# Chunked attention, a two-dimensional DFT and an MLP on one core: the PSUM banks divided among the three, and attention regrouped

## The chip, the cores and the metric

The kernel runs on one core of a Trainium2 chip. The metric is the device time of one execution in microseconds, as the median of several. Times before: 495.82, 498.5 and 500.54 us, median 498.5.

## What is computed

The reference first does attention in chunks of 32 positions, each with 16 positions to its left, 8 to its right and 8 memory positions, over 4 batches, 8 heads, 768 positions and a head size of 64. The heads side by side are x (4 x 768 x 512), and then:

```python
X = np.fft.fft(x, axis=1)
X = np.fft.fft(X, axis=2)
u = x + np.real(X).astype(np.float32)
mu = np.mean(u, axis=-1, keepdims=True)
var = np.mean((u - mu) ** 2, axis=-1, keepdims=True)
un = (u - mu) / np.sqrt(var + 1e-06)
ch = np.maximum(un @ w_ch1, 0.0) @ w_ch2        # 512 -> 2048 -> 512
return (u + ch).astype(np.float32)
```

## The kernel before

**Attention** (emit_pair, line 222) works on a pair of heads, 4 pairs a batch, 16 in all. The loads of q, k and v go through SP's queue (emit_loads, lines 105 to 120) into buffers that alternate: two for q and k, four for v (two pairs). POOL casts q and k to bf16 (lines 231, 233) and copies the overlap of v (line 237). PE transposes q and k (lines 242, 247) into one PSUM tile trp, ACT copies them out as qT and kT (lines 244, 252). PE then makes the scores of both heads in 24 matmuls (line 259) into two tiles sc0 and sc1 of two banks each; for each head ACT takes the exponential in two instructions (line 266), PE multiplies with v, in 12 products over tile xa (line 271; a product in fp32 shows as two matmul records), and DVE divides by the sum of weights (lines 274, 276) into xsb, which holds x of the batch. There are two xsb buffers: attention of batch b+2 writes into the one that the MLP of batch b reads last (line 379).

**The Fourier stage** (emit_fx, line 281), called so below, folds x by its symmetries on DVE (lines 290 to 299: zy, pq, ff), splits it into two fp16 parts hi (ACT, line 303) and lo (DVE, line 304), and does the DFT over positions as 60 matmuls of 193 columns into ps (lines 312, 319), which ACT and DVE take out as up and dn (lines 326 to 329). Then comes a loop kt over 6 blocks of 128 positions (line 333): 8 matmuls of the DFT over channels into pm (line 341), DVE adds x (xsb, line 345), does the statistics (lines 347, 348) and subtracts the mean (un, line 350), PE transposes un into tp (line 353), DVE copies it to unT (line 354). pm of kt 0 to 2 reads up, that of kt 3 to 5 reads dn. POOL makes rstd from the variances at the end (lines 356, 357).

**The MLP** (emit_mlp, line 360) runs over two halves of 384 positions. For each half there are 16 groups ht of 4 matmuls into ph (line 368), each followed by relu on ACT into hT (line 371), then 3 blocks of 16 matmuls into pc (line 376), each followed by osb on DVE (line 379) and an output DMA on SP's queue (line 381). The first half of positions needs unT of kt 0 to 2 alone.

**Order and buffers.** The order in which instructions stand on each engine is made by a scheduler that goes by a model of times and, among what could run, by the order of the text: attention 0, Fourier 0, attention 1, Fourier 1, MLP 0, attention 2, Fourier 2, MLP 1 and so on. On the chip every engine and every queue then keeps that order. A tile takes its buffer in the order of the text as well. The 8 banks of PSUM are divided so: trp, sc0 and sc1 share two buffers of two banks under the tag "sc" (4 banks), xa has one bank, and the tag "acc" of the pool fps has three, which the tiles mps, ps, pm, tp, ph and pc share. The weights of the MLP are loaded by eight DMAs on POOL's queue (emit_weights, line 204), in the text behind pair 2.

Of the kernel before, what the change touches and what calls it, by code (L numbers as in the profile page):

```python
# [10 lines left out]
FP32 = mybir.dt.float32  # L11
# [24 lines left out]
def kernel(  # L36
# [15 lines left out]
    P = 128  # L52
# [21 lines left out]
    fps = ctx.enter_context(tc.tile_pool(name="fx_ps", bufs=3, space=bass.MemoryType.PSUM))  # L74
# [147 lines left out]
    def emit_pair(n):  # L222
        b, pr = seq[n]
        h = 2 * pr
        if b not in xs:
            xs[b] = apool.tile([P, NST, DM], FP32, tag="xsb", bufs=2, name=f"xsb{b}")
        xb = xs[b]
        emit_loads(n)
        qb = apool.tile([QP, RB, 2, D], BF16, tag="qb", bufs=2)
        kb = apool.tile([KP, RB, 2, D], BF16, tag="kb", bufs=2)  # L230
# [31 lines left out]
        for hh in range(2):
            v1 = va[(2 * n + hh) % NV]
            e1 = apool.tile([P, NT, 64], FP32, tag="e1", bufs=3)
            for c in range(2):
                nc.scalar.activation(e1[:, :, ts(c, 32)], sc[hh][:, :, ts(c, 32)], AFT.Exp,  # L266
                                     bias=mbias[:, c:c + 1], scale=1.0 / math.sqrt(D))
            xa = aps.tile([P, NST, 66], FP32, tag="xa", bufs=1)
# [116 lines left out]
    for i in range(HP):  # L385
        emit_pair(i)
        if i == HP - 2:
            emit_weights()
# [37 lines left out]
```

## Time and profile before

| | us |
|---|---|
| times of three runs | 495.82, 498.5, 500.54 |
| the profiled execution, its own time | 500.56 |
| its span, first to last instruction | 498.6 |
| PE busy in the span | 340.6 (68%) |
| DVE busy | 207.1 (42%) |
| ACT busy | 150.6 (30%) |
| POOL busy | 90.8 (18%) |
| mean granted clock of PE | 0.808 |

PE is the matmul engine, PEld its weight loads, DVE the vector engine, ACT the one for functions, POOL and SP two more that also issue DMAs. "L341" is line 341 of the kernel before; lines move by up to 21 in the kernel after. [...] A busy PE is not a PE at its peak, since matmuls overlap: a matmul's duration is longer than the distance to the next. A matmul record of xa is half a product. All times in the rows are microseconds from the start of the span, unless marked ns.

### The profile page before, as it was taken

Reading aid. Unit: us, or ns where it says so; the run is one execution under the profiler, and the core shown is the slowest. Engines: PE = TensorE matmul, PEld = TensorE weight load, DVE = VectorE, ACT = ScalarE, POOL = GpSimd, SP = SyncE. Lnnn points to the kernel's source line nnn. Section 1 sums busy time; section 2 is a strip of 40 time slices with the busy share of each in tenths; the row PEclk is TensorE's granted clock in tenths of the full one; section 3 lists DMA queues with packets and bytes.
Section 4 is the critical chain, followed back from the end, with each engine's and each line's share of the span. In section 5 each row is a group of like instructions: output and inputs, shape, how many; then the busy total and the mean of one; then the engine's idle time right before and its main releaser. Section 6 shows DMA issues by size and latency. Waiting matters only on the chain.

```text
span 498.6 us, 6910 instructions
## 1 busy us (share of the span) xinstructions
PE 340.6 (68%) x2848; PEld 221.8 (44%) x2848; DVE 207.1 (42%) x365; ACT 150.6 (30%) x258; POOL 90.8 (18%) x99
## 2 busy tenths in 40 slices
PE   1045526766556669996557458997535559999996
PEld 1044415655444445554545235454523335555452
DVE  7911189564595450103186651103495550101101
ACT  2444242213423115233442005160312006244160
POOL 9715157005520013002422001000100010000000
PEclk9999999676556569999756558999757559999999
DMA  9639994332633005104130000102100000101101
GB/s 168 98 91 186 217 185 75 82 77 62 157 77 73 0 1 128 63 21 108 45 79 22 0 0 1 42 22 82 38 0 0 1 0 1 63 21 43 43 21 63
DMA packets 42022, 30.65 MB, mean 61 GB/s; under 512 B 30216, under 2 KB 32264, under 8 KB 41992
## 3 DMA queue, kind: packets, MB, share of 16 engines
q1 hardware_dynamic: 39304, 26.03, 22.7%
q0 software_dynamic: 2688, 4.19, 4.7%
q8 instruction: 22, 0.36, 0.3%
q14 instruction: 8, 0.07, 0.0%
HBM read 28.11 MB, written 6.29 MB: 69 GB/s over the span
## 4 chain that ended last, share of the span: by engine, by line
PE 57%; DVE 22%; DMA 7%; issue 6%; ACT 4%; SPq 2%; POOL 2%; POOLq 0%; ACTq 0%; DVEq 0%
PE ph L368 17%; PE pc L376 17%; PE pm L341 7%; DMA kf<-in_k_dram 6%; PE xa L271 5%; PE ps L312 5%; DVE xsb L345 3%; DVE st L347 3%; PE tp L353 3%; DVE zy L290 2%; DVE lo L304 2%; DVE un L350 2%; DVE xsb L276 1%; PE sc L259 1%; SPq L116 1%
## 5 line engine op out<-in xcount | busy, mean ns | idle before, releaser
L371 ACT ACTIVATE hT<-ph 128x384 f16<-128x384 f32 x128 | 62.9, 491 | 130.8 <-PE ph L368 130.3
L368 PE MATMUL ph<-unT,w_sb 128*128 128x384 f16 x512 | 87.1, 332 | 0.0
L376 PE MATMUL pc<-w_sb,hT 128*128 128x512 f16 x384 | 84.2, 379 | 0.0
L379 DVE SCALAR_TENSOR_TENSOR osb<-pc,rstd,xsb 128x512 f32<-128x512 f32 x24 | 18.0, 751 | 151.6 <-PE pc L376 151.6
L368 PEld LDWEIGHTS <-w_sb 128*128 128x128 f16 x512 | 51.0, 100 | 35.0 <-issue 2.7
L271 PE MATMUL xa<-va,e 128*64 128x65 f32 x768 | 43.9, 285 | 30.4 <-issue 13.2
L376 PEld LDWEIGHTS <-hT 128*128 128x128 f16 x384 | 37.6, 98 | 44.4
L271 PEld LDWEIGHTS xa<-va,e 128*64 128x64 f32 x768 | 38.6, 193 | 36.2 <-issue 22.0
L237 POOL COPY va<-va 32x768 f32<-32x768 f32 x32 | 32.5, 1029 | 100.8 <-DMA va<-in_v_dram 100.1
L266 ACT ACTIVATE e<-sc,mbias 128x384 f32<-128x384 f32 x64 | 32.4, 581 | 48.1 <-PE xa L271 31.1
L353 PE MATMUL tp<-ident_h,un 128*128 128x128 f16 x96 | 13.7, 293 | 39.9 <-DVE un L350 39.8
L312 PE MATMUL ps<-cosS,hi 128*128 128x193 f16 x48 | 15.8, 358 | 25.3 <-ACT hi L303 25.3
L356 POOL TENSOR_SCALAR rstd<-mu_s 128x6 f32<-128x6 f32 x4 | 2.0, 491 | 166.8 <-DVE mu_s L348 166.8
L244 ACT COPY qT<-trp 128x768 bf16<-128x768 bf16 x16 | 12.8, 800 | 62.5 <-PE trp L242 62.5
L259 PE MATMUL sc<-qT,kTb 64*128 64x64 bf16 x384 | 14.1, 224 | 25.0 <-ACT kTb L252 23.8
L353 PEld LDWEIGHTS <-un 128*128 128x128 f16 x96 | 7.8, 125 | 47.4 <-DVE un L350 47.0
L274 DVE RECIPROCAL zs<-xa 128x6 f32<-128x6 f32 x32 | 6.2, 194 | 51.6 <-PE xa L271 51.6
L231 POOL CAST qb<-qf 96x1024 bf16<-96x1024 f32 x16 | 18.7, 1166 | 46.8 <-PE trp L242 41.7
L345 DVE TENSOR_TENSOR xsb<-pm,xsb 128x512 f32<-128x512 f32 x24 | 16.6, 692 | 24.5 <-PE pm L341 24.3
L312 PEld LDWEIGHTS <-hi 128*128 128x128 f16 x96 | 12.7, 139 | 27.7 <-ACT hi L303 26.8
L326 ACT CAST up<-ps 128x386 f16<-128x386 f32 x16 | 9.5, 596 | 49.4 <-PE ps L312 37.8
L259 PEld LDWEIGHTS <-kTb 64*128 64x128 bf16 x384 | 11.0, 116 | 30.1 <-ACT kTb L252 26.6
(92 smaller groups left out, 455.7 us busy)
## 6 DMA issues: line engine op xcount, KB each, us to landing
qf<-in_q_dram SPq DMA_DIRECT2D x16, 384.0 KB
kf<-in_k_dram SPq DMA_DIRECT2D x16, 384.0 KB
out_dram<-osb SPq DMA_DIRECT2D x24, 256.0 KB
va<-in_v_dram SPq DMA_DIRECT2D x32, 144.0 KB
w_sb<-in_moe_w_ch_dram POOLq DMA_DIRECT2D x8, 512.0 KB, 14.0
va<-in_v_dram SPq DMA_DIRECT2D x32, 48.0 KB
va<-in_mem_v_dram SPq DMA_DIRECT2D x32, 24.0 KB
mkf<-in_mem_k_dram SPq DMA_DIRECT2D x1, 64.0 KB
```

What stands on the lines that cost most here:

```text
L231: nc.gpsimd.tensor_copy(qb.rearrange("p j h d -> p h j d"), qf[n % NS].rearrange("p h (j d) -> p h j d", j=RB))
L237: nc.gpsimd.tensor_copy(v1[96:128, 0:NT, 0:D], v1[0:32, 1:NB, 0:D])
L259: nc.tensor.matmul(sc[hh][:, t, :], kT[r0:r0 + 64, t * BS:t * BS + P], qT[r0:r0 + 64, ts(t, 64)], start=True, stop=True, tile_position=(r0 ...
L266: nc.scalar.activation(e1[:, :, ts(c, 32)], sc[hh][:, :, ts(c, 32)], AFT.Exp, bias=mbias[:, c:c + 1], scale=1.0 / math.sqrt(D))
L271: nc.tensor.matmul(xa[rr:rr + 64, t // 2, 0:65], e1[:, t, :], v1[:, t, 0:65], start=True, stop=True)
L312: nc.tensor.matmul(ps[:, sp, :], part[:, ab, sp * 3 + st, :], tab[:, sp, st, :], start=(st == 0 and i == 0), stop=(st == 2 and i == 1))
L341: nc.tensor.matmul(pm[:, par, :], lhs, rhs[:, par, :], start=(im == 0), stop=(im == 3))
L345: nc.vector.tensor_tensor(uv, pm, uv, ALU.add)
L353: nc.tensor.transpose(tp[:, dt, :], un[:, ts(dt, P)], ident_h)
L368: nc.tensor.matmul(ph[:, 0:384], w1_sb[:, dt, ts(ht, P)], unT[:, dt, sh * 384:(sh + 1) * 384], start=(dt == 0), stop=(dt == NDT - 1))
L371: nc.scalar.activation(hT[:, ht, :], ph[:, 0:384], AFT.Relu)
L376: nc.tensor.matmul(pc, hT[:, ht, ts(stl, P)], w2_sb[:, ht, :], start=(ht == 0), stop=(ht == NHT - 1))
```

## The change

Three things. The pool fps has two buffers a tag instead of three, and ph and pc get a tag of their own, "mlp"; so the Fourier stage and the MLP each have two banks. The transposes of q and k move into a function emit_keys, which is called for pair n+1 ahead of emit_pair for pair n; they have a tag "tr" with one bank, which trq and trk use in turn. And a pair is done in two halves g of 6 blocks for both heads at once: one sc tile (tag "sc", one buffer of two banks, a bank a head), two exps, 12 products into one xa tile, one division. The counts of instructions on each engine stay what they were. PSUM is then: tr 1, sc 2, xa 1, acc 2, mlp 2.

```diff
-    fps = ctx.enter_context(tc.tile_pool(name="fx_ps", bufs=3, space=bass.MemoryType.PSUM))
+    fps = ctx.enter_context(tc.tile_pool(name="fx_ps", bufs=2, space=bass.MemoryType.PSUM))
...
-    def emit_pair(n):
+    qT_of, kT_of = {}, {}
+
+    def emit_keys(n):
...
-        trp = aps.tile([P, 2, 1024], BF16, tag="sc", bufs=2)
+        trq = aps.tile([P, S], BF16, tag="tr", bufs=1, name="trq")
...
+        trk = aps.tile([P, RB * KP], BF16, tag="tr", bufs=1, name="trk")
...
+        qT_of[n], kT_of[n] = qT, kT
+
+    def emit_pair(n):
...
-        sc = [aps.tile([P, NT, 64], FP32, tag="sc", bufs=2, name=f"sc{hh}") for hh in range(2)]
-        for t in range(NT):
-            for hh in range(2):
-                r0 = 64 * hh
-                nc.tensor.matmul(sc[hh][:, t, :], kT[r0:r0 + 64, t * BS:t * BS + P],
...
-        for hh in range(2):
-            v1 = va[(2 * n + hh) % NV]
-            e1 = apool.tile([P, NT, 64], FP32, tag="e1", bufs=3)
-            for c in range(2):
-                nc.scalar.activation(e1[:, :, ts(c, 32)], sc[hh][:, :, ts(c, 32)], AFT.Exp,
...
-            xa = aps.tile([P, NST, 66], FP32, tag="xa", bufs=1)
-            for t in range(NT):
-                rr = 64 * (t % 2)
-                nc.tensor.matmul(xa[rr:rr + 64, t // 2, 0:65], e1[:, t, :], v1[:, t, 0:65],
-                                 start=True, stop=True)
...
+        qT, kT = qT_of.pop(n), kT_of.pop(n)
+        for g in range(2):
+            sc = aps.tile([P, 2, 8, 64], FP32, tag="sc", bufs=1, name="sc")
+            for t6 in range(6):
+                t = 6 * g + t6
+                for hh in range(2):
+                    r0 = 64 * hh
+                    nc.tensor.matmul(sc[:, hh, t6, :], kT[r0:r0 + 64, t * BS:t * BS + P],
+                                     qT[r0:r0 + 64, ts(t, 64)], start=True, stop=True,
+                                     tile_position=(r0, 0))
+            e1 = apool.tile([P, 2, 6, 64], FP32, tag="e1", bufs=3, name="e1")
+            for half in range(2):
+                nc.scalar.activation(e1[:, :, :, ts(half, 32)], sc[:, :, 0:6, ts(half, 32)],
+                                     AFT.Exp, bias=mbias[:, half:half + 1],
+                                     scale=1.0 / math.sqrt(D))
+            xa = aps.tile([P, 3, 2, 66], FP32, tag="xa", bufs=1, name="xa")
+            for st in range(3):
+                for hh in range(2):
+                    v1 = va[(2 * n + hh) % NV]
+                    for half in range(2):
+                        t6 = 2 * st + half
+                        nc.tensor.matmul(xa[64 * half:64 * half + 64, st, hh, 0:65],
+                                         e1[:, hh, t6, :], v1[:, 6 * g + t6, 0:65],
+                                         start=True, stop=True)
...
-                ph = fps.tile([P, 512], FP32, tag="acc", name="ph")
+                ph = fps.tile([P, 512], FP32, tag="mlp", name="ph")
...
-                pc = fps.tile([P, DM], FP32, tag="acc", name="pc")
+                pc = fps.tile([P, DM], FP32, tag="mlp", name="pc")
...
+    def emit_attention(b):
+        for i in range(HP):
+            n = b * HP + i
+            if n + 1 < B * HP:
+                emit_keys(n + 1)
+            emit_pair(n)
+            if n == HP - 2:
+                emit_weights()
```

The scheduler makes another order of this. The first place is on PE, in the kt loop of batch 1; tp_1421 and tp_1442 (before) or tp_1423 and tp_1444 (after) are the transposes of two steps that follow each other. Before:

```order
L353 MATMUL tp_1421<-ident_h_125,un_1419 128x128
L341 LDWEIGHTS dn_1279
L341 MATMUL pm_1427<-cosD_148,dn_1279 128x256
...
L341 MATMUL pm_1427<-sinD_150,dn_1358 128x256
L353 LDWEIGHTS un_1440
L353 MATMUL tp_1442<-ident_h_125,un_1440 128x128
```

After, where pc_1811 and pc_1831 are tiles of the MLP of batch 0:

```order
L367 MATMUL tp_1423<-ident_h_125,un_1421 128x128
L355 LDWEIGHTS up_1322
L355 MATMUL pm_1429<-cosD_148,up_1322 128x256
...
L355 MATMUL pm_1429<-nsinD_149,up_1401 128x256
L390 LDWEIGHTS hT_1694
L390 MATMUL pc_1811<-w2_sb_189,hT_1694 128x512
...
L390 MATMUL pc_1831<-w2_sb_189,hT_1694 128x512
L367 LDWEIGHTS un_1442
L367 MATMUL tp_1444<-ident_h_125,un_1442 128x128
```

Between pm of one step and tp of the same block there stood nothing; now there stand 13 matmuls of pc (1 of pc_1811 and 12 of pc_1831).

The second place is on ACT, from the second half of the MLP of batch 0 to the first of batch 1. Before, the relus of a half stand together:

```order
L371 ACTIVATE hT_1650<-ph_1735 128x384
L371 ACTIVATE hT_1650<-ph_1741 128x384
L266 ACTIVATE e1_2067<-sc0_2041,mbias_133 128x12x32 x2
L266 ACTIVATE e1_2086<-sc1_2042,mbias_133 128x12x32 x2
L244 COPY qT_2119<-trp_2120 128x768
```

After, the casts of the Fourier stage (hi, up), the exps (e1) and the copies of attention stand among them:

```order
L385 ACTIVATE hT_1694<-ph_1761 128x384
L317 CAST hi_1305<-ff_1301 128x1536
L385 ACTIVATE hT_1694<-ph_1767 128x384
L385 ACTIVATE hT_1694<-ph_1773 128x384
L275 ACTIVATE e1_1901<-sc_1888,mbias_133 128x12x32 x2
L385 ACTIVATE hT_1694<-ph_1779 128x384
L385 ACTIVATE hT_1694<-ph_1785 128x384
L340 CAST up_1322<-ps_1309 128x2x193
```

What moved are the relus: of the 128 in the kernel, the first 96 (batches 0 to 2) have left their place behind the Fourier stage of the next batch and stand beside it.

The third place is on PE, where the first ps of batch 1 is. Before, xa of the next attention is beside it:

```order
L312 MATMUL ps_1265<-cosS_146,hi_1261 128x193
L312 MATMUL ps_1283<-sinS_147,hi_1261 128x193
L271 MATMUL xa_1872<-va0_80,e1_1869 64x65 x12
L312 LDWEIGHTS lo_1262
L312 MATMUL ps_1265<-cosS_146,lo_1262 128x193
```

After:

```order
L326 MATMUL ps_1309<-cosS_146,hi_1305 128x193
L326 MATMUL ps_1327<-sinS_147,hi_1305 128x193
L382 MATMUL ph_1779<-unT_765,w1_sb_188 128x384
...
L382 MATMUL ph_1785<-unT_765,w1_sb_188 128x384
L284 MATMUL xa_1904<-va0_80,e1_1901 64x65
L326 MATMUL ps_1309<-cosS_146,lo_1306 128x193
```

The wait for lo is filled with two groups of ph of batch 0 and a first product of xa.

## Rows read from the trace of the kernel before

**Rows 1.** The page, busy time of each engine in the span.
```profile
PE 340.6 (68%) x2848; PEld 221.8 (44%) x2848; DVE 207.1 (42%) x365; ACT 150.6 (30%) x258; POOL 90.8 (18%) x99
```

**Rows 2.** Busy time by windows: us, PE, PEld, DVE, ACT, POOL, granted clock, DMA.
```profile
250.00:301.00 51.00, 28.59 (x202) 20.46 (x199) 35.26 (x54) 8.99 (x12) 6.33 (x6) 0.53 0.10 25
301.00:344.00 43.00, 43.00 (x228) 22.50 (x227) 4.18 (x6) 15.72 (x32) 1.35 (x1) 0.97 0.08 31
344.00:361.00 17.00, 9.89 (x209) 8.61 (x208) 6.77 (x17) 5.64 (x10) 2.47 (x3) 0.82 0.23 57
452.00:498.00 46.00, 42.41 (x229) 22.10 (x226) 5.26 (x7) 15.72 (x32) 0.00 (x0) 1.00 0.10 40
```

**Rows 3.** Timeline, kt 2 and 3 of batch 2: start, us, instruction, idle before.
```profile
284.97 0.69 DVE L345 TENSOR_TENSOR xsb<-pm,xsb 128x512 f32<-128x512 f32 x1 [1.28 <-PE pm L341]
...
286.64 0.48 DVE L350 TENSOR_SCALAR un<-xsb,mu_s 128x512 f16<-128x512 f32 x1
...
287.18 0.60 PE L353 MATMUL tp<-ident_h,un 128*128 128x128 f16 x4 [2.25 <-DVE un L350]
...
289.53 0.69 DVE L345 TENSOR_TENSOR xsb<-pm,xsb 128x512 f32<-128x512 f32 x1 [1.28 <-PE pm L341]
```

**Rows 4.** Timelines of DVE and PE, start of the Fourier stage of batch 2.
```profile
251.22 1.76 DVE L290 TENSOR_TENSOR zy<-xsb 128x1536 f32<-128x1536 f32 x1
...
258.96 0.34 PE L312 MATMUL ps<-cosS,hi 128*128 128x193 f16 x1 [1.49 <-ACT hi L303]
...
266.02 0.25 PE L319 MATMUL ps<-cosS,hi 128*1 128x193 f16 x1
266.11 0.24 PE L319 MATMUL ps<-cosS,lo 128*1 128x193 f16 x1
```

**Rows 5.** The chain that ended last: start, us, what.
```profile
101.31 0.89 PE pm L341 x8
...
105.16 1.21 PE pm L341 x8
...
287.79 1.72 PE pm L341 x8
...
323.32 10.40 PE ph L368 x64
333.72 10.36 PE pc L376 x48
...
484.05 10.37 PE pc L376 x48
```

**Rows 6.** Timeline, attention of batch 2 behind the MLP of batch 0.
```profile
229.70 1.05 ACT L266 ACTIVATE e<-sc,mbias 128x384 f32<-128x384 f32 x2 [12.24 <-PE xa L271]
...
230.59 0.92 PE L271 MATMUL xa<-va,e 128*64 128x65 f32 x24 [0.94 <-PE xa L271]
...
231.44 0.51 PE L242 MATMUL trp<-ident_b,qb 96*128 96x96 bf16 x8
...
235.13 0.52 PE L259 MATMUL sc<-qT,kTb 64*128 64x64 bf16 x24
```

**Rows 7.** Timeline of PE, attention of batch 0.
```profile
42.15 0.82 PE L242 MATMUL trp<-ident_b,qb 96*128 96x96 bf16 x8
...
51.98 0.82 PE L242 MATMUL trp<-ident_b,qb 96*128 96x96 bf16 x8
...
60.99 1.57 PE L271 MATMUL xa<-va,e 128*64 128x65 f32 x24 [1.86 <-DMA va<-in_mem_v_dram]
```

**Rows 8.** The page, DMA issues: KB each, median us to landing.
```profile
w_sb<-in_moe_w_ch_dram POOLq DMA_DIRECT2D x8, 512.0 KB, 14.0
```

**Rows 9.** The page, groups of the MLP: busy, mean ns of one, idle before.
```profile
L371 ACT ACTIVATE hT<-ph 128x384 f16<-128x384 f32 x128 | 62.9, 491 | 130.8 <-PE ph L368 130.3
L368 PE MATMUL ph<-unT,w_sb 128*128 128x384 f16 x512 | 87.1, 332 | 0.0
L379 DVE SCALAR_TENSOR_TENSOR osb<-pc,rstd,xsb 128x512 f32<-128x512 f32 x24 | 18.0, 751 | 151.6 <-PE pc L376 151.6
```

More of the change, by code (lines that the diff above doesn't have):

```diff
@@ L220, in emit_mem_keys @@
         nc.vector.tensor_copy(mkT, mps)
-    def emit_pair(n):
+    qT_of, kT_of = {}, {}
+    def emit_keys(n):
         b, pr = seq[n]
[L224 to L227, printed above, removed]
         emit_loads(n)
-        qb = apool.tile([QP, RB, 2, D], BF16, tag="qb", bufs=2)
-        kb = apool.tile([KP, RB, 2, D], BF16, tag="kb", bufs=2)
+        qb = apool.tile([QP, RB, 2, D], BF16, tag="qb", bufs=2, name="qb")
+        kb = apool.tile([KP, RB, 2, D], BF16, tag="kb", bufs=2, name="kb")
         nc.gpsimd.tensor_copy(qb.rearrange("p j h d -> p h j d"),
@@ L238, in emit_pair @@
         kT = kTb[n % NKT]
-        qT = apool.tile([P, S], BF16, tag="qT", bufs=2)
-        trp = aps.tile([P, 2, 1024], BF16, tag="sc", bufs=2)
+        qT = apool.tile([P, S], BF16, tag="qT", bufs=2, name="qT")
+        trq = aps.tile([P, S], BF16, tag="tr", bufs=1, name="trq")
         for j in range(RB):
-            nc.tensor.transpose(trp[:, 0, j * QP:(j + 1) * QP],
+            nc.tensor.transpose(trq[:, j * QP:(j + 1) * QP],
                                 qb[:, j].rearrange("p h d -> p (h d)"), ident_b[0:QP, 0:QP])
         nc.scalar.copy(qT.rearrange("p (a j) -> p a j", j=RB),
-                       trp[:, 0, 0:S].rearrange("p (j a) -> p a j", j=RB))
+                       trq.rearrange("p (j a) -> p a j", j=RB))
+        trk = aps.tile([P, RB * KP], BF16, tag="tr", bufs=1, name="trk")
         for j in range(RB):
-            nc.tensor.transpose(trp[:, 1, j * KP:(j + 1) * KP],
+            nc.tensor.transpose(trk[:, j * KP:(j + 1) * KP],
                                 kb[:, j].rearrange("p h d -> p (h d)"), ident_b[0:KP, 0:KP])
@@ L262, in emit_pair @@
[L262 to L277 removed]
+            strided(trk, 0, [[8, NB], [1, 8], [KP, RB]]))
@@ new lines, in emit_keys @@
+        qT_of[n], kT_of[n] = qT, kT
+    def emit_pair(n):
+        b, pr = seq[n]
+        h = 2 * pr
+        if b not in xs:
+            xs[b] = apool.tile([P, NST, DM], FP32, tag="xsb", bufs=2, name=f"xsb{b}")
+        xb = xs[b]
+        qT, kT = qT_of.pop(n), kT_of.pop(n)
[22 more added lines that the diff above has]
+                                         start=True, stop=True)
+            zs = apool.tile([P, 3, 2], FP32, tag="zs", bufs=3, name="zs")
+            nc.vector.reciprocal(zs, xa[:, :, :, 64])
+            nc.vector.tensor_tensor(
+                xb[:, 3 * g:3 * g + 3, h * D:(h + 2) * D].rearrange("p s (h d) -> p s h d", h=2),
+                xa[:, :, :, 0:D], zs.unsqueeze(3).to_broadcast([P, 3, 2, D]), ALU.mult)
@@ L383 @@
     HP = H // 2
+    def emit_attention(b):
[6 more added lines that the diff above has]
+                emit_weights()
     emit_mem_keys()
[L385 to L388, printed above, removed]
+    emit_keys(0)
+    emit_attention(0)
     emit_fx(0)
@@ L391 @@
         if b + 1 < B:
-            for i in range(HP):
-                emit_pair((b + 1) * HP + i)
+            emit_attention(b + 1)
             emit_fx(b + 1)
```

8 lines of the change are left out of this document (removed).

## The prediction

> **What bounds the kernel now.** I read the page's busy shares first: PE is busy for 340.6 us of the span, 68%, the other engines less [rows 1], so no engine fills the span and the stages have to be looked at one by one. The table of windows does that for one batch [rows 2]. In the Fourier stage of batch 2 (250 to 301 us) PE is busy 28.6 of 51 us at a granted clock of 0.53, and DVE 35.3. In the MLP of batch 1 (301 to 344) PE is full, at 0.97, and DVE does 4.2 us. In the attention of batch 3 (344 to 361) PE has 9.9 of 17 us. So the stages have opposite limits and stand one behind the other: the Fourier stage is a chain PE to DVE to PE, the MLP is PE alone, and the last 46 us are again MLP alone.
>
> The timeline shows the chain. One step of the kt loop (line 333) goes from the start of xsb at 284.97 to the next at 289.53, 4.56 us; PE starts tp at 287.18, after 2.25 us of idling for un, which DVE ended at 287.12 (286.64 + 0.48) [rows 3]. Ahead of the loop stand 7.7 us of DVE and ACT, zy at 251.22 to the first ps at 258.96 [rows 4]. From that ps to the end of the pm of kt 3 (just ahead of the xsb at 289.53, which reads it: its pm is the first that reads dn) it takes 30.6 us [rows 3, 4]. The MLP of a batch needs unT of kt 0 to 2 alone to begin, but its PSUM tiles come from the same three "acc" banks as the Fourier tiles of the next batch, in the order of the text; so it stands behind that whole stage.
>
> **Prices on PE.** [...] At the fast level: 64 ph matmuls 10.40 us, 0.1625 each; 48 pc 10.36, 0.216 each [rows 5]; 12 products of xa 0.92, 8 transposes 0.51, 24 sc 0.52 [rows 6]; ps 0.09 each (266.02 to 266.11) [rows 4].
>
> **What the change does, part by part.**
>
> *Attention alone (batch 0).* No instruction is added: 24 sc, 24 xa products, 4 exps, 16 transposes a pair as before. What changes is the order: two halves with one sc tile, so the second sc half waits for the exps of the first. Before, a pair takes 9.83 us (trp at 42.15 and at 51.98), and the last xa ends at 62.6 [rows 7]. In the new order the key transposes of pair n+1 still stand right ahead of its sc, since trk has to wait for the copy of trq out of the one "tr" bank; only the query half has moved under xa. Of the steps between, what goes is one exp wait and the qT wait, what comes is the wait of the second sc half: I count 8.9 us a pair, so 3 us less over the first four pairs, attention 0 ends near 60. The bounds are no gain (62.6) and 2 us a pair (54).
>
> *Queues.* On POOL the eight weight loads now stand behind the casts and va copies of pair 3, some 10 us later; a load lands in 14.0 us [rows 8], and the first MLP comes at 100, so this costs nothing unless the loads take over 40 us. On SP the outputs of the MLP now stand between the loads of q and k of the next pairs. These loads are issued one pair, thus 10 us of PE work or more, ahead of their use; the xa at 60.99 had waited 1.86 us for one [rows 7]. I take nothing here and keep 2 us a batch for the range.
>
> *From the end of attention 0 to the first MLP.* In the new order ph of batch 0 stands behind the pm of kt 3. Before, that pm ends at 106.4 (105.16 + 1.21) [rows 5], 43.8 us after attention. The same way in batch 2, without attention between, takes 7.7 + 30.6 = 38.3 [rows 3, 4]. I take 41, and the first ph at 101.
>
> *The cycle.* From here on the MLP of batch b fills PE under the attention and the Fourier stage of batch b+1. I cut the new PE order into three stretches a cycle, from the first ph of one batch to that of the next. *A*: kt 3 to 5 of the Fourier stage, three steps. At the fast level a step is shorter by 0.83 of pm and some 0.1 of tp, 3.6; so 10.8 to 13.7, I take 12. PE has 9.2 to 9.9 us of work there, which fits under it. *B*: the main part of the MLP with attention between. By counts from the order and the prices above: cycle 0 has 94 ph, 48 pc, 46 xa, 36 sc and 32 transposes, 32.0 us; cycle 1 has 110, 57, 55, 58 and 32, 37.7; cycle 2 has 102, 65, 48, 48 and 16, 36.4. *C*: the first ps to the pm of kt 3 of the next batch, 30.6 before; at the fast level three pm groups are shorter by 0.9 each with tp, the second 22 ps by 0.07 each, 4.4 together, and three osb of 0.75 [rows 9] come to DVE inside the chain, 2.2: 28.4. PE has 16 to 24 us of work there, and nothing ready for the rest.
>
> *What the split costs.* ph now has two banks where it had three. A bank is held from the first of 4 matmuls to the end of relu: 3 x 0.1625 + 0.33 (mean of an ph matmul) + 0.49 relu [rows 9], with handovers of 0.06 as from un to tp (287.12 to 287.18) [rows 3] on both sides 1.43 us, where two groups of PE work are 1.30. So 0.06 us a group, 1.4 to 1.7 us in each B. ACT also does two exps of 1.05 together [rows 6] and the qT and kT copies between the relus. Each of these can hold ph back by its length less the PE work beside it: between 0 and 8 us in a B (about eight such pieces), I take 3, since sc and xa of the same pair stand beside most of them.
>
> [...]
>
> *The end.* The last MLP has 39 ph under kt 3 to 5 (12 us), then 89 ph and 96 pc, 35.2 with 1.3 for the banks, 36.5. Behind the last pc the span had 4.2 us left (498.6 less 484.05 + 10.37) [rows 5], and keeps them.
>
> **The sum**, against the profiled execution (500.56 us, span 498.6, so 2.0 outside): first ph 101.3; cycle 0 12 + 32.0 + 4.4 + 28.4 = 76.8; cycle 1 12 + 37.7 + 4.7 + 28.4 = 82.8; cycle 2 12 + 36.4 + 4.5 + 28.4 = 81.3; end 12 + 36.5 + 4.2 = 52.7. Together 394.9, with what lies outside 396.9. The profiled execution stood 2.1 above the median of 498.5, so 395 for the median. Before, the way from the pm of kt 3 of batch 0 to the end took 392 us; now it takes 294. The 98 us are not removed work: they are three MLPs of 41.5 us, of which some 25 to 30 each now lie under the chains of the next batch, and PE matmuls that run at the fast level because PE idles less.
>
> **The rivals.** *R1, the cover is better*: fast steps in A (10.8), no ACT stalls in B, the osb in DVE's gaps in C (26), first stretch 38.3. That is 1.2 x 4 + 3 x 3 + 2.4 x 3 + 2.7 less, 24 us: 371. For it: DVE idles 1.28 a step for pm [rows 3]. Against it: ACT and DVE work in order, and each has more kinds of work in a row than before.
>
> *R2, PE's queue gives the chains' waits to the MLP*: the order is fixed, so an sc, xa or tp that comes later than it was placed for stops the ph behind it. Then A keeps 13.7, C 33 (30.6 and the osb), B has 8 of ACT stalls, and 2 more for late loads: 13.3 a cycle and 4 more at the start and the end, some 44: 439. For it: the 2.25 us a step that tp waits for un even now [rows 3]; against it, each such wait has PE work placed ahead of it in the new order.
>
> *R3, slower*: the MLP loses the fast level. It has it before because nothing interrupts it: 0.97 to 1.00 granted, where the Fourier stage with its idle steps has 0.53 [rows 2]. Interleaved, the MLP has the steps' idling in its middle. [...] Against it: the attention of batch 3 with 7 of 17 us idle still has 0.82 [rows 2], and B has next to no idling. [...]
>
> *R4, no change*: the order overlaps on paper, but loads or ACT hold every cycle to its old length of some 111 us (51 + 43 + 17) [rows 2]; about 490.
>
> **How the numbers follow.** My forecast, 380 to 412 by the stalls in B and the steps: 0.55. R1 0.2, R2 0.2, R3 0.02, R4 0.03. The range leaves out half of R1 below and about a third of R2 with R3 and R4 above: 372 to 434. Within 1% is about what a measurement of this kernel can tell from no change: faster 0.96, same 0.02, slower 0.02.
>
> **What would show it right or wrong.** Windows of the changed kernel: no stretch of 40 us with PE full and DVE nearly idle but the last; first ph near 101 us, then cycles of 77 to 83; granted clock over 0.9 in B; ph groups 0.65 to 0.71 apart where nothing stands between; kt steps of 3.6 to 4.6 us. Cycles of 90 or more with PE waiting on ACT's relu or exps say R2; ph matmuls 0.32 us apart with a low clock say R3; a first ph at 106 or later says that the loads or the pair order were wrong.

## The result, and the profile after

The kernel after takes 374.92 us (median of 4 runs, 373.94 to 378.14); the kernel before, run beside it, 497.16 (494.35 to 500.54). The ratio is 0.755, 95% interval 0.748 to 0.762: faster by about 122 us. The prediction had said 395, in a range of 372 to 434. The profiled execution of the kernel after takes 373.94 us, with a span of 372.2.

The page of the kernel after, busy times and three groups of the MLP, to set beside [rows 1, 9]:

```profile
PE 301.9 (81%) x2848; PEld 187.8 (50%) x2848; DVE 196.2 (53%) x365; ACT 148.6 (40%) x258; POOL 84.3 (23%) x99
...
L382 PE MATMUL ph<-unT,w_sb 128*128 128x384 f16 x512 | 96.0, 330 | 1.3 <-DVE osb L393 0.8
L385 ACT ACTIVATE hT<-ph 128x384 f16<-128x384 f32 x128 | 61.9, 494 | 76.8 <-PE ph L382 76.8
...
L393 DVE SCALAR_TENSOR_TENSOR osb<-pc,rstd,xsb 128x512 f32<-128x512 f32 x24 | 17.9, 748 | 51.5 <-PE pc L390 51.5
```

The work on PE hasn't become less (the same 2848 matmuls), yet PE is busy for 302 us where it was 341: the same matmuls run at the higher clock level more of the time (the mean granted clock, a share of PE's full clock in the trace, is 0.980, where it was 0.808). The relus, which waited 130.3 us for ph, now wait 76.8, and osb waits 51.5 us for pc where it waited 151.6.

The kernel after by windows, columns as in [rows 2], cut at the stretches of the prediction. The first row is most of attention 0, the second the first stretch; then come A, B, C for three cycles, and the end (A, and the rest):

```profile
30.00:59.90 29.90, 19.61 (x288) 16.65 (x288) 6.67 (x17) 12.13 (x20) 12.73 (x16) 1.00 0.74 142
59.90:96.70 36.80, 20.07 (x256) 16.45 (x256) 30.51 (x46) 12.62 (x18) 9.92 (x9) 0.97 0.88 169
96.70:106.80 10.10, 10.10 (x120) 6.66 (x119) 7.20 (x18) 5.95 (x12) 0.40 (x1) 0.94 0.40 77
106.80:142.60 35.80, 34.32 (x308) 19.06 (x308) 13.37 (x20) 17.89 (x33) 11.59 (x13) 1.00 0.25 70
142.60:167.90 25.30, 24.84 (x213) 15.82 (x214) 20.48 (x37) 7.93 (x13) 1.65 (x2) 1.00 0.17 50
167.90:178.40 10.50, 9.90 (x146) 7.06 (x146) 8.40 (x20) 6.01 (x12) 3.03 (x4) 1.00 1.03 194
178.40:219.60 41.20, 40.41 (x368) 22.19 (x367) 14.25 (x24) 22.00 (x42) 11.97 (x13) 1.00 0.34 80
219.60:244.60 25.00, 22.35 (x235) 15.22 (x235) 21.14 (x39) 7.34 (x11) 3.07 (x4) 1.00 0.30 82
244.60:255.20 10.60, 10.57 (x135) 7.45 (x136) 7.61 (x19) 6.29 (x12) 1.94 (x3) 1.00 0.58 133
255.20:294.10 38.90, 38.55 (x327) 20.67 (x328) 12.73 (x19) 19.65 (x38) 5.53 (x7) 1.00 0.09 29
294.10:320.90 26.80, 19.62 (x137) 12.55 (x137) 19.91 (x34) 3.87 (x5) 0.00 (x0) 0.85 0.08 30
320.90:331.50 10.60, 10.49 (x69) 6.22 (x67) 7.02 (x14) 4.42 (x9) 0.65 (x2) 0.89 0.01 2
331.50:372.20 40.70, 36.31 (x187) 17.77 (x184) 4.93 (x7) 11.30 (x23) 1.16 (x1) 0.98 0.10 39
```

The stretches with PE full and DVE nearly idle [rows 2] are gone but for the last one. In the three B windows (from 106.8, 178.4 and 255.2) PE is busy for 96 to 99% while DVE does 13 to 14 us and ACT 18 to 22. The cycles, from first ph to first ph, are 71.2 us (96.7 to 167.9), 76.7 and 76.3.

Timelines of the kernel after (ACT, PE, POOL and DVE; columns as in [rows 3]): attention 0, the start of the Fourier stage of batch 1, one kt step of it, and the last ph:

```profile
23.84 0.83 ACT L252 COPY kTb<-trk 128x832 bf16<-128x832 bf16 x1
...
40.40 0.82 PE L241 MATMUL trq<-ident_b,qb 96*128 96x96 bf16 x8
...
44.46 0.50 PE L270 MATMUL sc<-qT,kTb 64*128 64x64 bf16 x12 [0.94 <-ACT kTb L252]
...
49.20 2.42 POOL L206 DMA_DIRECT2D w_sb<-in_moe_w_ch_dram  x4
49.54 0.82 PE L241 MATMUL trq<-ident_b,qb 96*128 96x96 bf16 x8
...
58.30 1.57 PE L284 MATMUL xa<-va,e 128*64 128x65 f32 x24 [0.98 <-DVE xsb L289]
...
67.90 0.34 PE L326 MATMUL ps<-cosS,hi 128*128 128x193 f16 x1 [8.04 <-ACT hi L317]
...
142.59 0.26 PE L326 MATMUL ps<-cosS,hi 128*128 128x193 f16 x1 [1.09 <-ACT hi L317]
...
156.09 0.69 DVE L359 TENSOR_TENSOR xsb<-pm,xsb 128x512 f32<-128x512 f32 x1
...
159.61 0.69 DVE L359 TENSOR_TENSOR xsb<-pm,xsb 128x512 f32<-128x512 f32 x1 [0.45 <-PE pm L355]
160.22 0.74 DVE L393 SCALAR_TENSOR_TENSOR osb<-pc,rstd,xsb 128x512 f32<-128x512 f32 x1
...
163.67 0.69 DVE L359 TENSOR_TENSOR xsb<-pm,xsb 128x512 f32<-128x512 f32 x1 [0.45 <-PE pm L355]
...
347.11 10.53 PE L382 MATMUL ph<-unT,w_sb 128*128 128x384 f16 x60 [0.19 <-DVE osb L393]
357.48 0.81 PE L390 MATMUL pc<-w_sb,hT 128*128 128x512 f16 x3
```

A pair of attention 0 takes 9.14 us (40.40 to 49.54), and the last xa ends at 59.87. The weight loads start at 49.20. From the first ps of batch 1 to its first xsb it is 13.5 us (142.59 to 156.09), and this kt step takes 4.06 us (159.61 to 163.67) with an osb inside it, where the step of [rows 3] took 4.56 without one. The 60 ph at 347.11 have nothing beside them and take 10.37 us to the next pc, 0.69 for each group of four.

The chain that ended last in the kernel after (start, us, what):

```profile
246.96 0.87 PE pm L355 x8
...
285.27 0.85 PE xa L284 x24
...
314.67 1.72 PE pm L355 x8
```

The pm of a kt takes 0.87 us with the MLP beside it, and 1.72 at 314.67 (the next, at 319.24, takes 1.71), where the order has no MLP work left to put beside it and PE idles in each step, as it did before: from 310.0 to 320.9 us it is busy for 5.85, at a granted clock of 0.63.

### The profile page after: what moved, and what is told of

The parts are those of the page before. It is cut to its first block, busy times and chain, and to the rows that moved or that the text cites. A ratio compares the mean times of both kernels' runs of the same rounds, so it can differ in the third digit from the quotient of the medians.

```text
span 372.2 us, 6899 instructions
## 1 busy us (share of the span) xinstructions
PE 301.9 (81%) x2848; PEld 187.8 (50%) x2848; DVE 196.2 (53%) x365; ACT 148.6 (40%) x258; POOL 84.3 (23%) x99
## 4 chain that ended last, share of the span: by engine, by line
PE 63%; DVE 27%; ACT 6%; issue 3%; ACTq 0%; DVEq 0%
PE pc L390 19%; PE ph L382 19%; PE xa L284 10%; PE pm L355 5%; PE sc L270 3%; ACT e L275 3%; PE ps L326 2%; DVE zy L304 2%; PE tp L367 2%; DVE lo L318 2%; DVE st L361 2%; DVE xsb L359 2%; DVE un L364 2%; DVE up L341 2%; ACT hi L317 2%
## 5 line engine op out<-in xcount | busy, mean ns | idle before, releaser
L382 PE MATMUL ph<-unT,w_sb 128*128 128x384 f16 x512 | 96.0, 330 | 1.3 <-DVE osb L393 0.8
L385 ACT ACTIVATE hT<-ph 128x384 f16<-128x384 f32 x128 | 61.9, 494 | 76.8 <-PE ph L382 76.8
L390 PE MATMUL pc<-w_sb,hT 128*128 128x512 f16 x384 | 89.5, 379 | 0.0
L382 PEld LDWEIGHTS <-w_sb 128*128 128x128 f16 x512 | 48.2, 98 | 37.3 <-issue 9.3
L236 POOL COPY va<-va 32x768 f32<-32x768 f32 x32 | 29.6, 934 | 115.8 <-DMA va<-in_v_dram 115.2
L393 DVE SCALAR_TENSOR_TENSOR osb<-pc,rstd,xsb 128x512 f32<-128x512 f32 x24 | 17.9, 748 | 51.5 <-PE pc L390 51.5
L284 PEld LDWEIGHTS xa<-va,e 128*64 128x64 f32 x768 | 34.0, 161 | 20.8 <-issue 13.9
L243 ACT COPY qT<-trq 128x768 bf16<-128x768 bf16 x16 | 12.8, 799 | 49.3 <-PE trq L241 49.2
L359 DVE TENSOR_TENSOR xsb<-pm,xsb 128x512 f32<-128x512 f32 x24 | 16.6, 693 | 10.9 <-PE pm L355 10.9
L232 POOL CAST kb<-kf 104x1024 bf16<-104x1024 f32 x16 | 17.8, 1110 | 4.8 <-DMA kf<-in_k_dram 3.3
L252 ACT COPY kTb<-trk 128x832 bf16<-128x832 bf16 x16 | 13.6, 852 | 12.9 <-PE trk L247 12.9
L326 PE MATMUL ps<-cosS,hi 128*128 128x193 f16 x48 | 10.3, 264 | 10.3 <-ACT hi L317 9.9
L367 PE MATMUL tp<-ident_h,un 128*128 128x128 f16 x96 | 9.9, 228 | 10.6 <-DVE un L364 10.3
```

The costliest lines, as they stand in the source:

```text
L232: nc.gpsimd.tensor_copy(kb.rearrange("p j h d -> p h j d"), kf[n % NS].rearrange("p h (j d) -> p h j d", j=RB))
L236: nc.gpsimd.tensor_copy(v1[96:128, 0:NT, 0:D], v1[0:32, 1:NB, 0:D])
L284: nc.tensor.matmul(xa[64 * half:64 * half + 64, st, hh, 0:65], e1[:, hh, t6, :], v1[:, 6 * g + t6, 0:65], start=True, stop=True)
L326: nc.tensor.matmul(ps[:, sp, :], part[:, ab, sp * 3 + st, :], tab[:, sp, st, :], start=(st == 0 and i == 0), stop=(st == 2 and i == 1))
L359: nc.vector.tensor_tensor(uv, pm, uv, ALU.add)
L382: nc.tensor.matmul(ph[:, 0:384], w1_sb[:, dt, ts(ht, P)], unT[:, dt, sh * 384:(sh + 1) * 384], start=(dt == 0), stop=(dt == NDT - 1))
```

## The experiments

The kernel before ran beside each of these; the ratios are to it, and are what is compared.

| kernel | edit in a few words | median us | ratio, 95% interval |
|---|---|---|---|
| after | | 374.9 | 0.755 (0.748 to 0.762) |
| e1_shared | split undone, 4 shared banks | 497.0 | 1.000 (0.995 to 1.005) |
| e2_split21 | before, split 2 + 1 alone | 466.7 | 0.939 (0.930 to 0.948) |
| e3_split12 | before, split 1 + 2 alone | 393.1 | 0.793 (0.786 to 0.800) |
| e4_no_ahead | keys not ahead | 389.8 | 0.787 (0.781 to 0.794) |
| e4b_loads | keys not ahead, loads ahead | 386.9 | 0.779 (0.774 to 0.785) |
| e10_e4_wlate | keys not ahead, weights later | 382.0 | 0.772 (0.768 to 0.776) |
| e12_wlate | weights later | 377.9 | 0.763 (0.758 to 0.769) |
| e5_mlp3 | banks 1 + 3 | 382.6 | 0.773 (0.768 to 0.777) |
| e6_heads | attention head by head | 383.7 | 0.775 (0.770 to 0.780) |
| e7_osb | osb on ACT and POOL | 377.7 | 0.763 (0.759 to 0.767) |
| e9_tab0 | tables built later | 367.8 | 0.743 (0.737 to 0.749) |
| e14_kk | tables later still | 371.5 | 0.750 (0.746 to 0.754) |

### Is it the split? (e1_shared, e2_split21, e3_split12)

e1_shared is the kernel after with the tag "mlp" undone and four banks for all (pc as ph):

```diff
-    fps = ctx.enter_context(tc.tile_pool(name="fx_ps", bufs=2, space=bass.MemoryType.PSUM))
+    fps = ctx.enter_context(tc.tile_pool(name="fx_ps", bufs=4, space=bass.MemoryType.PSUM))
...
-                ph = fps.tile([P, 512], FP32, tag="mlp", name="ph")
+                ph = fps.tile([P, 512], FP32, tag="acc", name="ph")
```

> The kernel after with one edit undone: ph and pc take the tag "acc" again, which now has four banks for Fourier stage and MLP together; attention is that of the kernel after. Theory (the split gives nearly all of the gain, since it alone lets the MLP of a batch be placed beside the next batch's Fourier stage): the MLP stands behind the whole next Fourier stage again, a stretch of some 43 us with PE full and DVE nearly idle is back in every batch, and only attention's 1 to 3 us a batch are kept: 480 to 495 us. Rival (the regrouped attention, or keys one pair ahead, or the one bank more, carries a good part): 400 to 460 us.

Measured: 497.0 us, ratio 1.000. Without the split nothing is left of the gain, though this kernel has a bank more for the two stages together than the kernel before (four shared, not three), the keys ahead and the regrouped attention. The window of its first MLP:

```profile
172.40:213.90 41.50, 41.50 (x228) 21.95 (x226) 4.18 (x6) 16.02 (x33) 4.24 (x4) 1.00 0.20 61
```

PE is full for all of 41.5 us and DVE does 4.2, as in [rows 2]. So without the tags of their own there is no overlap; that they are enough for most of it is for e3_split12 to show. The time lies 2 us above the theory's range: in the trace the first ph comes at 172.4 us, 13 us earlier than in the kernel before (185.6), but the medians don't show it, and where it goes stays open.

e2_split21 is the kernel before with two Fourier banks and one for the MLP (pc as ph), its attention untouched:

```diff
-    fps = ctx.enter_context(tc.tile_pool(name="fx_ps", bufs=3, space=bass.MemoryType.PSUM))
+    fps = ctx.enter_context(tc.tile_pool(name="fx_ps", bufs=2, space=bass.MemoryType.PSUM))
...
-                ph = fps.tile([P, 512], FP32, tag="acc", name="ph")
+                ph = fps.tile([P, 512], FP32, tag="mlp", bufs=1, name="ph")
```

> The kernel before with the split alone and its old attention: two banks for the Fourier stage, one for ph and pc (all that the old attention leaves). Theory (the split gives the overlap, and the MLP needs two banks, since with one a group of ph, 0.65 us, can't begin before the relu of the group ahead, 0.49 us and its handovers, is done): the relu and handovers, some 0.7 us, are added to each of 32 ph groups a batch, about 22 us, of which A and C, where PE has time to spare, hide perhaps a third; so about 15 us a batch more than the kernel after, 425 to 450 us. Rival (only the order matters, one bank does): below 395 us.

Measured: 466.7 us, above the theory's range. Timeline of e2_split21, PE in its last MLP:

```profile
432.59 0.81 PE L368 MATMUL ph<-unT,w_sb 128*128 128x384 f16 x4 [0.58 <-ACT hT L371]
...
433.98 0.81 PE L368 MATMUL ph<-unT,w_sb 128*128 128x384 f16 x4 [0.58 <-ACT hT L371]
```

A group of ph comes every 1.39 us (432.59 to 433.98), PE idling 0.58 for the relu; with two banks it is 0.69. The price of the missing bank, 0.70 a group, was right. From the table of waits of e2_split21 (who waits for whom: us in total, times, longest):

```profile
PE ph L368 <- ACT hT L371: 48.1, 84, 1.8
...
PE pc L376 <- DVE osb L379: 14.0, 14, 2.1
```

PE waits for the relu 84 times, in 128 groups; so a third of the groups do have other work beside the wait, as was expected. By an estimate, 84 times 0.70, the relu costs 59 us. What the theory left out is that pc takes the same single bank: PE waits 14.0 us for osb ahead of pc, and 4.2 more ahead of ph. The kernel stands 92 us above the kernel after; the 15 that are left no run splits further, but e2_split21 also has the old attention and the early weights.

e3_split12 has it the other way round:

```diff
-    fps = ctx.enter_context(tc.tile_pool(name="fx_ps", bufs=3, space=bass.MemoryType.PSUM))
+    fps = ctx.enter_context(tc.tile_pool(name="fx_ps", bufs=1, space=bass.MemoryType.PSUM))
...
-                ph = fps.tile([P, 512], FP32, tag="acc", name="ph")
+                ph = fps.tile([P, 512], FP32, tag="mlp", bufs=2, name="ph")
```

> The kernel before with the split alone and its old attention, the other way round: one bank for the Fourier stage, two for ph and pc. Theory (the chains bound A and C, the MLP bounds B): in a kt step pm of the next block has to wait for the copy of unT, so pm and its handover no longer lie beside the statistics, some 1 us a step more, and ps has to wait for each copy of up; about 6 to 12 us a batch, where the MLP under it takes some of it back: 390 to 420 us. Rival (the three-way division with the regrouped attention is what counts, the old attention on four banks with the keys not ahead stalls PE): above 430 us. Second rival (the number of Fourier banks doesn't count): 372 to 382 us.

Measured: 393.1 us, as the theory has it. The old attention with the split alone has 103 of the 122 us. From the table of waits, first of e3_split12 and then of the kernel after:

```profile
DVE xsb L345 <- PE pm L341: 25.0, 24, 2.0
```

```profile
DVE xsb L359 <- PE pm L355: 10.9, 20, 1.3
```

With one bank pm of the next block can't start until unT is copied, and over the 24 kt DVE's first step waits 25.0 us for pm instead of 10.9.

### What gives the other 19 us? (e4_no_ahead, e4b_loads, e10_e4_wlate, e6_heads, e5_mlp3)

e4_no_ahead is the kernel after with the keys emitted right ahead of their own pair:

```diff
             n = b * HP + i
-            if n + 1 < B * HP:
-                emit_keys(n + 1)
+            emit_keys(n)
             emit_pair(n)
...
-    emit_keys(0)
```

> The kernel after with the transposes of q and k emitted right ahead of their own pair, not one pair ahead; tags and banks as after. Theory (the trq transposes under xa save one wait a pair in attention alone, 0 to 1.5 us a pair, and where the MLP stands beside attention PE has other work): first ph 0 to 5 us later, cycles the same within 2 us: 375 to 383 us. Rival (the keys ahead are what keeps PE from waiting in the stretches with MLP and attention): 390 us or more.

Measured: 389.8 us, against the theory and at the rival's bound. But the cycles aren't where most of it lies: its first ps comes at 77.3 us, 9.4 later than in the kernel after. Timelines of e4_no_ahead, POOL and PE:

```profile
38.30 2.42 POOL L206 DMA_DIRECT2D w_sb<-in_moe_w_ch_dram  x4
...
57.12 0.48 PE L284 MATMUL xa<-va,e 128*64 128x65 f32 x4 [1.26 <-ACT e L275]
...
62.74 1.35 PE L284 MATMUL xa<-va,e 128*64 128x65 f32 x20 [4.76 <-DMA va<-in_mem_v_dram]
...
108.59 1.17 PE L382 MATMUL ph<-unT,w_sb 128*128 128x384 f16 x3
```

An xa stops in its middle, at 57.6, and waits 4.8 us for va. Moving emit_keys moved two more things: the loads that it issues, and on POOL the casts and va copies of pair 3, which in the kernel after stand ahead of the weight loads. The weight loads begin at 49.20 us in the kernel after and at 38.30 here (36.64 in the kernel before).

e4b_loads takes the loads out of emit_keys and issues them one pair ahead again; against e4_no_ahead:

```diff
-        emit_loads(n)
...
+            if n + 1 < B * HP:
+                emit_loads(n + 1)
             emit_keys(n)
...
+    emit_loads(0)
```

> Like e4_no_ahead (transposes of q and k with their own pair), but the loads of q, k and v are issued one pair ahead, as in the kernel after. It tells apart the two things that moving the keys moved: the place of the loads in SP's queue, and that of the transposes on PE. Theory (the 15 us that e4_no_ahead lost to the kernel after, 9.4 of them ahead of the first Fourier stage, are loads that come a pair later: its xa waits for va there): attention 0 ends near 60 us again, 373 to 380 us. Rival (the transposes' place is what counts): 386 to 392 us, the pair period in attention 0 near 9.8 us.

Measured: 386.9 us, within the rival's 386 to 392. This theory falls: the interval overlaps that of e4_no_ahead, and xa waits for va at the same place, 4.85 us at 62.85. Timeline of PE in e4b_loads, the first ph of batches 0 and 1:

```profile
106.69 0.65 PE L381 MATMUL ph<-unT,w_sb 128*128 128x384 f16 x3
...
178.73 1.30 PE L381 MATMUL ph<-unT,w_sb 128*128 128x384 f16 x7
```

e10_e4_wlate leaves the loads and moves the weights; against e4_no_ahead:

```diff
-            if n == HP - 2:
+            if n == HP - 1:
                 emit_weights()
```

> e4_no_ahead with the weight loads emitted after pair 3 instead of pair 2; nothing else. In the traces the eight weight loads are issued on POOL's queue at 38.3 us in e4_no_ahead (36.6 in the kernel before) and at 49.2 in the kernel after, since there the casts and va copies of pair 3 stand ahead of them. Theory (the 9 us that e4_no_ahead loses ahead of the first Fourier stage are DMA: 4.2 MB of weights share the DMA engines with the v loads of pair 3, whose xa waits 4.8 us at 62.7): with the weights behind pair 3 attention 0 ends at 61 to 63 us, the first ps comes near 70, and the time is 375 to 382 us. Rival (the transposes of the keys one pair ahead are the cause): no change, 387 to 392 us.

Measured: 382.0 us, just past the end of what the theory said, 7.6 below e4_no_ahead by the ratios. Timelines of e10_e4_wlate, POOL and PE:

```profile
48.85 2.42 POOL L206 DMA_DIRECT2D w_sb<-in_moe_w_ch_dram  x4
...
57.81 1.57 PE L284 MATMUL xa<-va,e 128*64 128x65 f32 x24
...
98.31 1.78 PE L382 MATMUL ph<-unT,w_sb 128*128 128x384 f16 x8
...
173.25 1.47 PE L382 MATMUL ph<-unT,w_sb 128*128 128x384 f16 x8
```

The wait for va is gone, and the first ps comes at 70.6 us. So about half of what e4_no_ahead lost is the 4.2 MB of weights, which take the DMA engines from the last loads of va in attention 0. Of the other half, 8 us, some 2 are the place of the transposes in attention 0: trq no longer lies under xa, a pair takes 9.7 us instead of 9.14, and the last xa ends at 61.9 instead of 59.9. At the first ph (98.31) the kernel is 1.6 us behind the kernel after. The rest comes in the first two cycles, which in the traces take 74.9 us (98.31 to 173.25) and 79.5, where the kernel after has 71.2 and 76.7. In e4b_loads, whose transposes are late too but whose loads are a pair ahead, they take 72.0 (106.69 to 178.73) and 76.5. That speaks for the place of the loads, not of the transposes; it isn't shown, since no kernel here has the loads ahead and the weights late without the keys ahead.

e12_wlate makes the same edit on the kernel after:

```diff
-            if n == HP - 2:
+            if n == HP - 1:
                 emit_weights()
```

> The kernel after with the weight loads emitted after pair 3, so that they stand behind the casts and va copies of the first pair of batch 1 on POOL's queue, some 20 us later than in the kernel after. Theory (the loads of batch 1 then come sooner, but attention 1 has the whole first Fourier stage to be done in, and the first ph at 96.7 needs w1 landed): the same within 3 us, 372 to 378 us. Rival (the loads of batch 1 are late in the kernel after too, and hold PE in the first Fourier stage): 4 to 8 us off, 367 to 371 us. Second rival (the weights land too late for the first ph): 378 to 390 us.

Measured: 377.9 us, at the theory's upper end, its interval overlapping that of the kernel after. Weights at 61.9 us gain nothing over 49.2.

e6_heads is the kernel after with each head's 12 blocks done by themselves, exps, products and division likewise:

```diff
-        for g in range(2):
-            sc = aps.tile([P, 2, 8, 64], FP32, tag="sc", bufs=1, name="sc")
-            for t6 in range(6):
-                t = 6 * g + t6
-                for hh in range(2):
+        for hh in range(2):
+            sc = aps.tile([P, NT, 64], FP32, tag="sc", bufs=1, name="sc")
+            for t in range(NT):
...
```

> The kernel after with the regrouping of attention undone: one head after the other in one sc tile (12 blocks), the same banks, loads and keys one pair ahead. Theory (the regrouping gives nothing of its own: the same 24 scores, 24 products and 4 exps a pair, the same two waits of sc for the exps): 373 to 380 us, pair period in attention 0 9.0 to 9.4 us. Rival (scores of the two heads in turn on the two row halves of PE overlap, and head by head they don't): the 24 scores of a pair take about twice as long, 0.5 us a pair on PE and more ahead of each exp, 380 to 388 us.

Measured: 383.7 us: the rival. Timeline of PE in e6_heads, the scores of one head:

```profile
45.61 0.82 PE L269 MATMUL sc<-qT,kTb 64*128 64x64 bf16 x12 [0.94 <-ACT kTb L252]
```

12 scores of one head take 0.82 us; 12 that change heads at each matmul take 0.50 (the row at 44.46 of the kernel after), and in the kernel before 24 that do so 0.82 (at 45.65). The kernel puts two heads in turn on the two halves of PE's rows (tile_position), and there they overlap: 24 go in the time of one head's 12, 0.82 us. A pair takes 10.5 us in e6_heads (42.10 to 52.62), 1.4 more than in the kernel after: 0.6 of it are the scores, the rest is trq, which in this order stands behind xa again. So with one sc tile the regrouping is needed to keep what the kernel before had with two.

e5_mlp3 is the kernel after with its banks divided one and three (pc as ph):

```diff
-    fps = ctx.enter_context(tc.tile_pool(name="fx_ps", bufs=2, space=bass.MemoryType.PSUM))
+    fps = ctx.enter_context(tc.tile_pool(name="fx_ps", bufs=1, space=bass.MemoryType.PSUM))
...
-                ph = fps.tile([P, 512], FP32, tag="mlp", name="ph")
+                ph = fps.tile([P, 512], FP32, tag="mlp", bufs=3, name="ph")
```

> The kernel after with its four banks divided otherwise: one for the Fourier stage, three for ph and pc. Theory (one Fourier bank cost some 3 to 4 us a cycle in e3_split12; the third bank of the MLP takes back 0.05 us for each of 32 ph groups a batch, 1.6 us, only where PE is full): 380 to 388 us, ph groups at the end 0.65 us apart. Rival (the MLP's banks bound the cycle more than the chains): 365 to 373 us.

Measured: 382.6 us, as the theory has it. Timeline of PE in e5_mlp3, its last ph and pc:

```profile
355.43 10.56 PE L382 MATMUL ph<-unT,w_sb 128*128 128x384 f16 x64
365.83 10.52 PE L390 MATMUL pc<-w_sb,hT 128*128 128x512 f16 x48
```

64 ph take 10.40 us to the next pc, 0.65 a group, with three banks; with two it is 0.69. The third bank is worth 0.04 us a group. The second Fourier bank is worth more; the table of waits of e5_mlp3 has, where the kernel after has 10.9 us:

```profile
DVE xsb L359 <- PE pm L355: 27.1, 24, 2.0
```

By the ratios e4_no_ahead, e5_mlp3 and e6_heads lose 16, 9 and 10 us to the kernel after. That is more than the 19 which e3_split12 loses with its old attention and one Fourier bank, so these shares can't be added up.

### Can it be better? (e7_osb, e9_tab0, e14_kk)

e7_osb is the kernel after with osb taken off DVE:

```diff
-                nc.vector.scalar_tensor_tensor(osb, pc, rstd[:, st:st + 1], xb[:, st, :],
-                                               ALU.mult, ALU.add)
+                nc.scalar.mul(osb, pc, rstd[:, st:st + 1])
+                nc.gpsimd.tensor_tensor(osb, osb, xb[:, st, :], ALU.add)
```

> The kernel after with osb made by ACT (times rstd) and POOL (plus xsb) in two instructions instead of one on DVE. Theory (three osb of 0.75 us stand in DVE's chain in each of the stretches from the first ps to the pm of kt 3, and bound them): up to 2.2 us off each of three such stretches, 366 to 372 us. Rival (the osb lie in DVE's waits for pm and tp, and the bank of pc is held longer and ACT has 24 instructions more between its relus): 375 to 382 us.

Measured: 377.7 us: the rival. The steps without osb are shorter (3.51 us, the xsb at 233.13 to that at 236.64, against 4.06 with one in the kernel after), so an osb costs 0.55 us in a step. But from the first ps to the pm of kt 3 nothing is won: ACT, which now has the osb, is later with up, DVE waits 1.83 us for it at 230.35, and from the first ps of batch 2 to its first xsb it is 14.2 us (218.97 to 233.13) where the kernel after has 12.4 (219.64 to 232.01). There the osb lie in DVE's gaps.

e9_tab0 makes a function emit_tables of the lines that build the cosine and sine tables (160 to 199 of the kernel after), and calls it behind the first pair:

```diff
+    def emit_tables():
...
             emit_pair(n)
+            if n == 0:
+                emit_tables()
```

> The kernel after with the cosine and sine tables built behind the first pair in the text instead of ahead of it. In the kernel after the copy of the first pair's keys on ACT stands behind seven Sin instructions and the first scores come at 24.7 us, while the DMA engines are nearly idle from 19 to 30 us, since the loads of pair 2 wait for the va buffers of pair 0. Theory (attention 0 begins some 6 to 10 us earlier, and the loads then have the DMA engines to themselves): the first ps 4 to 8 us earlier, 367 to 371 us. Rival (the loads' rate sets the end of attention 0, or DVE's and ACT's work on the tables only moves into the pairs behind): 373 to 378 us.

Measured: 367.8 us, ratio 0.743 (0.737 to 0.749) against 0.755 (0.748 to 0.762): the fastest kernel here, by some 6 us; the two intervals still overlap, at 0.748. Timelines of e9_tab0, ACT and PE:

```profile
12.22 0.85 ACT L253 COPY kTb<-trk 128x832 bf16<-128x832 bf16 x1 [1.00 <-PE trk L248]
...
62.85 0.34 PE L327 MATMUL ps<-cosS,hi 128*128 128x193 f16 x1 [8.04 <-ACT hi L318]
```

The first pair's keys are copied at 12.22 us, not 23.84, and the first ps comes at 62.85, not 67.90: 5.05 us earlier; the span ends 7.3 earlier (364.9).

e14_kk, against e9_tab0:

```diff
-        kk = fpool.tile([P, 2, HD], FP32, tag="osb", bufs=3, name="kk")
+        kk = apool.tile([P, 2, HD], FP32, tag="e1", bufs=3, name="kk")
...
-            if n == 0:
+            if n == 1:
                 emit_tables()
```

> e9_tab0 with the tables behind the second pair in the text, and their first tile kk in a buffer of the tag e1, which comes free with the first pair's last product; so the tables can't be begun before that pair is done. In e9_tab0 the division of the first pair still stands behind the whole table arithmetic on DVE (first zs at 24.2 us, after 13.6 us of it), and its second exps behind two more table loads on ACT. Theory (the first pair's end sets the loads of the third pair, and the tables then lie under the wait for loads): the first pair is done near 19 us, pair 2 starts some 3 us earlier than in e9_tab0, the first ps comes at 58 to 61 us (62.9 there, 67.9 in the kernel after), 362 to 367 us. Rival (from pair 2 on the loads or ACT's tables hold it just as long): 366 to 371 us.

Measured: 371.5 us, no faster than e9_tab0 (0.750 against 0.743, the intervals overlap) and just above what the rival said. Timeline of PE in e14_kk:

```profile
37.85 0.45 PE L285 MATMUL xa<-va,e 128*64 128x65 f32 x2 [12.12 <-DVE xsb L290]
```

The tables' arithmetic now lies as one block on DVE between the two halves of the second pair, whose xa waits 12.1 us for the division. The first pair is done early (its last xa at 20.3 us), and the block was only moved.

## Why the prediction was right, and where it was off

The direction, the mechanism and the order of the terms were right: the MLP under the chains of the next batch, by the split (nothing of it without, e1_shared; 103 of 122 us by the split alone, e3_split12), and faster matmuls where PE idles less. The time came out 20 us below the forecast and below the forecast's own 380 to 412; what happened is nearly R1, the better cover (371), which had had a chance of 0.2. The median lies 3 us above the lower end of the range: the first stretch, A, B and C all erred to the same side, so the range held with little to spare. Point by point, against the profiled span:

| term | predicted us | measured us |
|---|---|---|
| end of attention 0 | 60 | 59.9 |
| first ph | 101.3 | 96.7 |
| A, three cycles and the end | 12 each | 10.1, 10.5, 10.6, 10.6 |
| B with bank waits and ACT stalls | 36.4, 42.4, 40.9 | 35.8, 41.2, 38.9 |
| C | 28.4 each | 25.3, 25.0, 26.8 |
| the last MLP behind A, and the tail | 36.5 + 4.2 | 40.7 |

The sum of 394.9 was 22.7 too much: 4.6 in the first stretch, 6.2 in A, 3.8 in B, 8.1 in C. (Its first term has a slip of its own: 60 and 41 make 101.0, not 101.3, and four pairs of 0.93 us less are 3.7, not 3.)

*The first stretch and the queues.* The step that failed here is "On POOL the eight weight loads now stand ... some 10 us later ... so this costs nothing". It cost nothing and it gave something, and I had priced only one side of it: I asked whether the weights come too late, not what their leaving makes room for. I had then taken 41 us for the stretch behind attention 0 from the kernel before (43.8), which has the early weights in it. With early weights e4_no_ahead still has 41.5 from the end of its last xa (67.1) to its first ph (108.59); with late ones, its only change, e10_e4_wlate has 36.4 (61.9 to 98.31), and the kernel after 36.8. The rows that could have told it stood there: the xa at 60.99 waiting 1.86 us for va [rows 7], with 4.2 MB of weights issued ahead of its loads.

*A.* The low bound of three fast steps, 10.8, was the value to take: PE's other work lies in the steps' waits, and a little less than that was measured.

*C.* Of 3.1 us too much (first cycle), 1.9 lie ahead of the loop: the first ps to the first xsb is 13.5 us, and was 16.9 in batch 2 of the kernel before (258.96 to 275.83). I had put 1.5 there, for 22 ps; but in batch 2 of the kernel before all but a few of the 60 ps stand 0.16 us apart (22 of them take 3.75 us at 270.35), and in the kernel after 0.085. An osb costs 0.55 us where it lies in a step (4.06 against 3.51) and nothing that shows ahead of the loop (e7_osb), less than the 0.75 each that made 2.2. In batch 3 C is 26.8, since the MLP work runs out and two steps fall back to 1.72 us of pm.

*B.* The counts and prices held within 2 us a stretch. The bank wait was put at 0.06 us a group and is 0.04 (e5_mlp3); with one bank it is 0.74 a group more than with three (e2_split21), where 0.7 was expected.

*Attention alone.* 8.9 us a pair was forecast, 9.14 measured.

*The rivals.* R2 (PE's queue gives the waits to the MLP) would have shown cycles of 90 us and more; they are 71 to 77, and ph waited 1.3 us in all. R3 (the MLP loses the fast level) is refuted: the granted clock is 1.00 in every B and C but the last C, and ph start 0.1625 us apart there as before. It even went the other way: filling the steps' idle time lifted the Fourier stage to the fast level (the 8 pm of a kt 0.87 us at 246.96, and 1.72 at 314.67, where the steps idle again). R4 (no change) is refuted by the time; e1_shared comes near R4's time (497.0 against 490), but from an order without overlap, not from loads or ACT.

## What to carry to other kernels

Where two stages with opposite limits share one rotation of buffers, the order in which tiles take them is a dependency; give each stage buffers of its own before looking for anything cleverer, and two each where the consumer's time is near that of the producer (with one for the MLP the kernel was 92 us slower here, most of it waits for that bank; a third was worth 0.04 us a group). When an edit moves a function, price the DMAs it moves in both directions: what comes later, and what finds the queues free because of it. And look at the start: tables that nothing reads before the first ps, at 67.90 us, stood ahead of the first pair.

## What was not expected of the hardware

*PE kept the fast level through short gaps.* In the last MLP of e2_split21 PE idles 0.58 us in every 1.39. The window of 15 such groups (columns as above):

```profile
428.37:449.70 21.33, 12.60 (x63) 6.04 (x63) 0.00 (x0) 7.35 (x15) 0.00 (x0) 1.00 0.03 13
```

PE is busy 12.6 of 21.3 us at a granted clock of 1.00, and its ph stay 0.1625 us apart, while the kt steps with idles of 2.25 us [rows 3] and an end of C with 0.85 in the mean have pm of 1.72. In the MLP the granted clock is near 1 on one, two or three banks: 1.00 in this window, 0.98 in the last row of the kernel after by windows, 0.97 and 1.00 in the two MLPs of [rows 2].

*The granted clock of a window isn't always the level that PE runs at.* From 30.0 to 59.9 us the kernel after has 1.00 by the windows, and yet the 24 records of xa take 1.57 us at 58.30, and 0.85 at 285.27. Early in the kernel the durations say the slow level and the column doesn't; so the first stretch has to be read from durations.

*The scores of two heads in turn* take half the time of one head's (24 in 0.82 us, where e6_heads has 12 in 0.82), which no row of the kernel before could show, since it always alternated.
